# Odd tiles of an expert move into a last step of three tiles, two arms of a branch in every expert step

## The chip, the cores and the metric

One core of one Trainium2 chip runs the whole program in one launch. The metric is the device time of that launch in microseconds (us). One execution was also profiled; its trace gives the start and duration of nearly every instruction. TensorE has two records for a matmul: PEld is the load of the stationary operand, PE the product. Every engine has its own instruction stream with its own branches; registers for the branches are loaded from a small table in SBUF.

## The reference

Attention with random features over 8 batches, 8 heads, 576 tokens of width 64, then a mixture of 8 experts, top 1, over the resulting 4608 tokens of width 512:

```python
x = attention(q, k, v, omega)             # [4608, 512], random-feature (linear) attention
probs = softmax(x @ w_gate)               # [4608, 8]
expert_idx = np.argmax(x @ w_gate, axis=1)
for e in range(8):
    xe = x[expert_idx == e]
    h = np.maximum(xe @ w1[e], 0.0)       # 512 -> 1024
    out[expert_idx == e] = gate_w * (h @ w2[e])   # 1024 -> 512
```

How many tokens an expert gets is known only at run time, so the program has the largest number of steps that could be needed, and leaves by branches.

## The kernel before

**Stages.** Up to about 271 us the core computes the attention, writes x to a DRAM table `token_rows` and counts tokens per expert. From 271 to 297 us it turns the counts into slots (`slots`), gathers the first tokens and computes the first pair of tiles in plain f32 (`fill`, `relu0`, `l20`). From 297 us to the end it runs expert steps.

**Tiles and steps.** The tokens of each expert are padded to tiles of 128. A step t takes two tiles of one expert, 256 tokens. In float32r each product is the sum of three: high part by high part, low weight by high token, high weight by low token. A step is, on TensorE:

1. L1 (`products`, line 869): 8 slices of the hidden width with 12 matmuls each of 128 x 256, 96 in all, into four PSUM banks `p_1`. After each bank ScalarE writes the high part `hh` (line 883) and VectorE the low part `hl` (line 887).
2. `begin(t+1)`: 8 transposes of the next step's gathered tokens (line 850); ScalarE and VectorE split them into `xh` and `xl`.
3. L2 (`l2`, lines 894 to 896): 24 matmuls of 128 x 512 for the first tile and 24 for the second; after each, ScalarE and VectorE scale half of the result by the gate, and GpSimd issues the indirect store to `out` (line 903).

The gathers are indirect DMAs on GpSimd (line 843), two for the step after the next, ahead of the stores.

**Odd tiles.** An expert with an odd number of tiles has a last step with one real tile. L1 still runs over all 256 columns; the second tile's L2 is left out by a branch (`when`, line 908) on a flag loaded in `reg` (line 830), on TensorE, VectorE, ScalarE and GpSimd. Steps 1 to 17 always run; from step 18 on each step is nested in an `If` (`tail`, line 949).

**Slots.** `slots` is a chain on VectorE: counts to tiles per expert, to offsets, to a slot number `f_tt` for each of 36 x 128 tokens, to a one-hot table `f_T` of 36 x NS columns; then 72 small matmuls (line 698) turn that into the token index of each slot, `idx`. While VectorE works on it, TensorE computes `fill(13)`: 13 of the first pair's 32 f32 products (line 797, two records each); ten are done earlier, the last nine by `fill(32)` behind the 72 matmuls. NS is 50. Behind `idx`, VectorE computes the flags (`plan`), splits w1 of the first expert (`split`, line 45) and the tokens of step 1, in that order.

The order of the instructions of each engine is the order in which the code is written.

Of the kernel before, what the change touches and what calls it, by code (L numbers as in the profile page):

```python
# [34 lines left out]
NS = 2 * NPR  # L35
# [376 lines left out]
class Routing:  # L412
# [190 lines left out]
    def head(self, nb, idx, flags):  # L603
# [8 lines left out]
        so, mb, T = t("so", [P, n, E], BF16), t("mb", [P, n]), t("T", [P, n, 2], BF16)  # L612

# [53 lines left out]
    def slots(self, wk, banks, idx, fill):  # L667
# [7 lines left out]
        cnt, c2, off, m = t("cnt", [P, E]), t("c2", [P, E]), t("off", [P, E]), t("m", [P, E, E])  # L675
        c1, tmp = t("c1", [1, E]), t("tmp", [1, E])
# [3 lines left out]
        nc.vector.tensor_scalar(out=tmp, in0=pn[:1, :E], scalar1=float(P - 1), scalar2=1.0 / P, op0=ALU.add, op1=ALU.mult)  # L680
        cb = c2.unsqueeze(1).to_broadcast([P, E, E])
        nc.vector.tensor_tensor(out=m, in0=self.low, in1=cb, op=ALU.mult)
        nc.vector.tensor_reduce(out=off, in_=m, axis=AX.X, op=ALU.add)
        so, tt = self.L.rearrange("p g s e -> p (g s) e"), t("tt", [P, NLT])
        nc.vector.tensor_tensor(out=so, in0=self.OH.rearrange("p g s e -> p (g s) e"),
                                in1=off.unsqueeze(1).to_broadcast([P, NLT, E]), op=ALU.mult)
        nc.vector.tensor_reduce(out=tt, in_=so, axis=AX.X, op=ALU.add)
        nc.vector.scalar_tensor_tensor(out=tt, in0=tt, scalar=2.0, in1=self.RT.rearrange("p g s -> p (g s)"),
                                       op0=ALU.mult, op1=ALU.add)
# [14 lines left out]
        nc.vector.tensor_scalar_add(tmp, tmp, FLOOR)  # L704
        nc.vector.tensor_scalar(out=c1, in0=tmp, scalar1=BIG, scalar2=-BIG, op0=ALU.add, op1=ALU.add)
        self.inc, self.off, self.c1, self.c2 = inc, off, c1, c2

    def plan(self, flags):
# [27 lines left out]
        nc.vector.scalar_tensor_tensor(out=en, in0=self.off[:1], scalar=2.0, in1=self.c1, op0=ALU.mult, op1=ALU.add)  # L736
        nc.vector.tensor_tensor(out=pick, in0=eq, in1=en.unsqueeze(1).to_broadcast([1, NQ, E]), op=ALU.mult)
        nc.vector.tensor_reduce(out=sb, in_=pick, axis=AX.X, op=ALU.add)
        nc.vector.scalar_tensor_tensor(out=sb, in0=self.iop[:1, :NQ], scalar=-2.0, in1=sb, op0=ALU.mult, op1=ALU.add)
        nc.vector.tensor_single_scalar(sb, sb, 1.5, op=ALU.is_gt)  # L740
        for i, a in ((0, ch), (1, nt), (2, act), (4, sb)):
            nc.vector.tensor_copy(flags[:, i, :], a)


class Experts:
# [3 lines left out]
    NC, NF, T2 = DM // P, F // P, 2 * P  # L749
    WE = (ET.DVE, ET.Activation, ET.SP)  # L750

    def __init__(self, tc, ctx, rt, xs, w1, w2, out, ident, ps):
        self.tc, self.nc, self.ctx, self.rt, self.ps, self.ident = tc, tc.nc, ctx, rt, ps, ident
        self.xs, self.w1, self.w2, self.out = xs, w1, w2, out
        cp = ctx.enter_context(tc.tile_pool(name="mo_a", bufs=1))
        self.w1s = cp.tile([P, self.NC, F], F32, name="w1s")
        self.w2s = cp.tile([P, self.NF, DM], F32, name="w2s")
        self.idx = cp.tile([P, NS], U32, name="idx")
        self.x0 = cp.tile([P, self.NC, self.T2], F32, name="x0")
        self.idx0 = cp.tile([P, 2], U32, name="idx0")  # L760
        self.flags = cp.tile([1, 5, NPR + 2], I32, name="flags")
# [5 lines left out]
        gt = cp.tile([P, 6], F32, name="gt")  # L767
        self.gt = [gt[:, i:i + 1] for i in range(6)]
# [71 lines left out]

    def gather(self, t):
        for i in range(2 * t, 2 * t + 2):
            self.nc.gpsimd.indirect_dma_start(out=self.xg[i % len(self.xg)], out_offset=None, in_=self.xs[:, :],
                                              in_offset=bass.IndirectOffsetOnAxis(ap=self.idx[:, i:i + 1], axis=0),
                                              bounds_check=NT - 1, oob_is_err=False)

    def turn(self, i, p):
        x = self.xg[i % len(self.xg)]
        for c in range(self.NC):
            self.nc.tensor.transpose(p[:, c * P:(c + 1) * P], x[:, c * P:(c + 1) * P], self.ident)  # L850
        self.nc.gpsimd.tensor_copy(self.gt[i % 6], x[:, DM:DM + 1])

    def xtrans(self, t):
        nc = self.nc
        for a in range(2):
            p = self.p_x[a]
            self.turn(2 * t + a, p)
            s = slice(a * P, (a + 1) * P)
            split_r(nc, self.xh[t % 2][:, :, s], self.xl[t % 2][:, :, s], p.rearrange("p (c t) -> p c t", t=P),
                    nc.scalar, nc.vector)  # L860

    def products(self, t, g, b):

        NC, T2 = self.NC, self.T2
        h, l = self.xh[t % 2], self.xl[t % 2]
        o = self.p_1[g][:, b * T2:(b + 1) * T2]
        f = slice((2 * g + b) * P, (2 * g + b + 1) * P)
        ops = [(w, h, c) for c in range(NC) for w in (self.w1h, self.w1l)] + [(self.w1h, l, c) for c in range(NC)]
        return [lambda w=w, x=x, c=c, n=n: self.nc.tensor.matmul(o, w[:, c, f], x[:, c, :], start=n == 0,  # L869
                                                               stop=n == len(ops) - 1)  # L870
                for n, (w, x, c) in enumerate(ops)]

    def l1(self, t, g):
        for b in range(2):
            for m in self.products(t, g, b):
                m()

    def hid(self, t, g):
        return (y[t % 2][:, 2 * g:2 * g + 2, :].rearrange("p f t -> p (f t)") for y in (self.hh, self.hl))

    def relu(self, t, g):
        a, b = self.hid(t, g)
        self.nc.scalar.activation(a, self.p_1[g], AF.Relu)  # L883

    def hlow(self, t, g):
        a, b = self.hid(t, g)
        self.nc.vector.scalar_tensor_tensor(out=b, in0=self.p_1[g], scalar=0.0, in1=a.bitcast(F32), op0=ALU.max,  # L887
                                            op1=ALU.subtract)

    def l2(self, t, a):  # L890
        nc, i, k = self.nc, 2 * t + a, slice(a * P, (a + 1) * P)
        h, l, p = self.hh[t % 2], self.hl[t % 2], self.p_2[a]
# [4 lines left out]
        self.store(i, p, self.idx)  # L897

    def store(self, i, p, idx):
        y, c = self.ys[i % 3], DM // 2  # L900
        self.nc.scalar.activation(y[:, :c], p[:, :c], AF.Copy, scale=self.gt[i % 6])  # L901
        self.nc.vector.tensor_scalar_mul(y[:, c:], p[:, c:], self.gt[i % 6])  # L902
        self.nc.gpsimd.indirect_dma_start(out=self.out[:, :], in_=y, in_offset=None, bounds_check=NT - 1,  # L903
                                          out_offset=bass.IndirectOffsetOnAxis(ap=idx[:, i:i + 1], axis=0),
# [21 lines left out]
    def step(self, t, following):  # L926
        for g in range(4):
            if t == 1:
                self.split(2, range(2 * g, 2 * g + 2))
            self.l1(t, g)  # L930
            self.relu(t, g)
            self.hlow(t, g)
        if t + 2 < NPR:
            self.gather(t + 2)
        if t == 1:
            self.next(0, 2)
        following()
        self.nc.gpsimd.drain()  # L938
        self.l2(t, 0)
        self.when(self.reg(4, t, 1, (ET.PE, ET.DVE, ET.Activation, ET.Pool)), lambda: self.l2(t, 1))  # L940
# [11 lines left out]
    def run(self, ctx):  # L952
# [6 lines left out]
        ring = lambda n, sh, dt, k: [cp.tile(sh, dt, name=f"{n}{i}") for i in range(k)]  # L959
        (self.w1h, self.w1l), (self.w2h, self.w2l) = (ring(n, [P, c, w], F32R, 2) for n, c, w in  # L960
                                                      (("w1p", NC, F), ("w2p", NF, DM)))
        self.ys = ring("ys", [P, DM], F32, 3)
        xg = ring("xgm", [P, ROW], F32, 2)
        for x in xg:
            nc.gpsimd.memset(x, 0.0)
        self.xg = self.xg + xg
        self.xh, self.xl = (ring(n, [P, NC, T2], F32R, 2) for n in ("xh", "xl"))
        self.h0 = cp.tile([P, NF, T2], F32, name="h0", tag="hh0")
        self.hh, self.hl = ([cp.tile([P, NF, T2], F32R, name=f"{n}{i}", tag=f"{n}{i}") for i in range(2)]
                            for n in ("hh", "hl"))  # L970

        rt.slots(cp, (self.p_2[0], self.p_x[0], self.p_x[1]), self.idx, lambda: self.fill(13))
# [9 lines left out]
        self.l20(1)  # L982
        self.gather(2)
        for t in range(1, NPL - 1):
# [3 lines left out]
        self.tail(NPL - 1)  # L988
# [45 lines left out]
```

## Time and profile before

| | before |
|---|---|
| time, median of 3 runs | 739.29 us (738.57 to 739.39) |
| the profiled execution's own time | 738.4 us |
| its span, first to last instruction | 736.7 us |
| mean granted TensorE clock | 0.998 |
| busy: PE / DVE / ACT / POOL | 719.9 / 377.9 / 327.5 / 245.7 us |
| expert steps in the trace | 19, two of them with one tile |

The span is 1.7 us short of the execution's own time, which lies at the lower edge of the timed runs; the median is 0.9 us above it. TensorE's records nearly touch each other from start to end, so "busy" for it says that it always had something in flight.

### The profile page before, as it was taken

Reading aid. Unit: us, or ns where it says so; the run is one execution under the profiler, and the core shown is the slowest. Engines: PE = TensorE matmul, PEld = TensorE weight load, DVE = VectorE, ACT = ScalarE, POOL = GpSimd, SP = SyncE. Lnnn points to the kernel's source line nnn. Section 1 sums busy time; section 2 is a strip of 40 time slices with the busy share of each in tenths; the row PEclk is TensorE's granted clock in tenths of the full one; section 3 lists DMA queues with packets and bytes.
Section 4 is the critical chain, followed back from the end, with each engine's and each line's share of the span. In section 5 each row is a group of like instructions: output and inputs, shape, how many; then the busy total and the mean of one; then the engine's idle time right before and its main releaser. Section 6 shows DMA issues by size and latency. Waiting matters only on the chain. (4 is left out here: it accounts for less than half of the span.)

```text
span 736.7 us, 18562 instructions
## 1 busy us (share of the span) xinstructions
PE 719.9 (98%) x7161; PEld 641.1 (87%) x7161; DVE 377.9 (51%) x848; ACT 327.5 (44%) x952; POOL 245.7 (33%) x446
## 2 busy tenths in 40 slices
PE   7999999999999999999999999999999999999996
PEld 6898988888888986898899988998898999889995
DVE  4689898899899887511222153221154217212210
ACT  6878878877778734411122152221152216112210
POOL 7555555555556521322022202122122122201121
PEclk9999999999999999999999999999999999999999
DMA  8944644627444422631011134111026115301000
GB/s 207 256 123 126 201 128 135 195 78 235 144 132 149 177 68 68 216 120 46 28 35 58 59 129 164 44 44 59 19 63 243 45 59 191 134 16 32 30 29 21
DMA packets 68347, 79.34 MB, mean 108 GB/s; under 512 B 27278, under 2 KB 51854, under 8 KB 68240
## 3 DMA queue, kind: packets, MB, share of 16 engines
q1 hardware_dynamic: 61136, 58.81, 25.8%
q0 software_dynamic: 6560, 19.03, 7.6%
q8 instruction: 59, 0.97, 0.6%
q14 instruction: 48, 0.39, 0.2%
q10 hardware_dynamic: 544, 0.13, 0.1%
HBM read 61.06 MB, written 19.55 MB: 109 GB/s over the span
## 5 line engine op out<-in xcount | busy, mean ns | idle before, releaser
L869 PE MATMUL p<-xh,w1p 128*128 128x256 f32 x1216 | 168.1, 280 | 0.3
L869 PEld LDWEIGHTS p<-xh,w1p 128*128 128x128 f32 x1216 | 154.8, 188 | 3.1 <-issue 1.6
L903 POOL DMA_INDIRECT out_dram<-ys,idx x38 | 39.2, 1032 | 347.1 <-DVE ys L902 305.3
L887 DVE SCALAR_TENSOR_TENSOR hl<-p,hh 128x512 fp32r<-128x512 f32 x76 | 52.3, 691 | 145.0 <-ACT hh L883 142.9
L894 PE MATMUL p<-w2p,hh 128*128 128x512 f32 x288 | 115.3, 400 | 0.3 <-PEq L908 0.3
L896 PE MATMUL p<-w2p,hl 128*128 128x512 f32 x288 | 113.6, 395 | 0.0
L895 PE MATMUL p<-w2p,hh 128*128 128x512 f32 x288 | 113.6, 394 | 0.0
L883 ACT ACTIVATE hh<-p 128x512 fp32r<-128x512 f32 x76 | 45.4, 598 | 151.3 <-PE p L869 149.1
L902 DVE TENSOR_SCALAR ys<-p,gt 128x256 f32<-128x256 f32 x38 | 18.3, 483 | 167.0 <-ACT ys L901 167.0
L901 ACT ACTIVATE ys<-p,gt 128x256 f32<-128x256 f32 x38 | 18.0, 474 | 179.2 <-PE p L896 85.3
L869 PE MATMUL p<-xl,w1p 128*128 128x256 f32 x608 | 96.1, 279 | 0.0
L185 ACT ACTIVATE kp<-pp,mx 128x128 f32<-128x128 f32 x256 | 76.2, 417 | 42.9 <-DVE mx L175 22.7
L869 PEld LDWEIGHTS p<-xl,w1p 128*128 128x128 f32 x608 | 82.1, 188 | 0.0
L175 DVE TENSOR_REDUCE mx<-pp 128x8 f32<-128x1024 f32 x64 | 77.0, 1215 | 7.6 <-PE pp L168 4.4
L185 ACT ACTIVATE qp<-pp,mx 128x128 f32<-128x128 f32 x256 | 78.4, 457 | 0.0
L202 POOL TENSOR_TENSOR k<-kp 128x256 f32<-128x256 f32 x64 | 46.7, 729 | 86.3 <-ACT kp L185 77.2
L168 PE MATMUL pp<-om_t,th 64*128 64x128 f32 x1024 | 70.7, 283 | 1.4 <-ACT qp L185 0.7
L168 PEld LDWEIGHTS pp<-om_t,th 64*128 64x128 f32 x1024 | 61.5, 187 | 9.8 <-issue 5.5
L896 PEld LDWEIGHTS p<-w2p,hl 128*128 128x128 f32 x288 | 54.0, 187 | 13.3
L894 PEld LDWEIGHTS p<-w2p,hh 128*128 128x128 f32 x288 | 54.0, 187 | 12.8 <-issue 0.5
L895 PEld LDWEIGHTS p<-w2p,hh 128*128 128x128 f32 x288 | 54.0, 188 | 12.4
L214 DVE COPY qt<-t 128x512 f32<-128x512 f32 x64 | 43.5, 680 | 2.9 <-PE t L212 2.9
(349 smaller groups left out, 1068.3 us busy)
## 6 DMA issues: line engine op xcount, KB each, us to landing
w1s<-in_moe_w_dram SPq DMA_DIRECT2D x5, 2048.0 KB, 9.0
w2s<-in_moe_w_dram SPq DMA_DIRECT2D x5, 2048.0 KB, 10.2
v<-in_v_dram SPq DMA_DIRECT2D x32, 256.0 KB, 5.3
token_rows<-xc SPq DMA_DIRECT2D x8, 1024.0 KB, 5.1
k<-in_k_dram SPq DMA_DIRECT2D x31, 256.0 KB, 5.2
q<-in_q_dram SPq DMA_DIRECT2D x31, 256.0 KB, 5.2
kr<-in_k_dram SPq DMA_DIRECT2D x16, 64.0 KB, 2.6
vz<-in_v_dram SPq DMA_DIRECT2D x16, 64.0 KB, 4.7
```

Of the source, the lines that this page charges most:

```text
L168: nc.tensor.matmul(pp[:, a, n, i, :], th[r, c], self.om[r, :], start=True, stop=True)
L175: nc.vector.tensor_reduce(out=mx[:, :, n], in_=s[("pp", h)][:, :, n], axis=AX.X, op=ALU.max, negate=True)
L185: nc.scalar.activation(x[:, j, :], pp[:, j % 2, n, j // 2, :], AF.Exp, bias=mx[:, j % 2, n, j // 2:j // 2 + 1])
L202: add = lambda o, x, y: nc.gpsimd.tensor_tensor(out=o, in0=x, in1=y, op=ALU.add)
L214: nc.vector.tensor_copy(qt.rearrange("p a b -> p (a b)"), pt)
L869: return [lambda w=w, x=x, c=c, n=n: self.nc.tensor.matmul(o, w[:, c, f], x[:, c, :], start=n == 0, stop=n == len(ops) - 1) for n, (w, x, ...
L883: self.nc.scalar.activation(a, self.p_1[g], AF.Relu)
L887: self.nc.vector.scalar_tensor_tensor(out=b, in0=self.p_1[g], scalar=0.0, in1=a.bitcast(F32), op0=ALU.max, op1=ALU.subtract)
L894: nc.tensor.matmul(p, h[:, c, k], self.w2h[:, c, :], start=c == 0, stop=False)
L895: nc.tensor.matmul(p, h[:, c, k], self.w2l[:, c, :], start=False, stop=False)
L896: nc.tensor.matmul(p, l[:, c, k], self.w2h[:, c, :], start=False, stop=c == self.NF - 1)
L903: self.nc.gpsimd.indirect_dma_start(out=self.out[:, :], in_=y, in_offset=None, bounds_check=NT - 1, out_offset=bass.IndirectOffsetOnAxis(a ...
```

## The change

The steps. A step has two tiles or three. An expert with an odd number of tiles (three or more) has its last three tiles in one step: the rounding of the tiles per expert to steps goes down where the count is odd. Each step loads a flag `two` on all five engines and takes one of two arms: the pair as before, or the three tiles (`third`, then L1 with 384 columns, then three times L2). The third tile has its own slot column (50 + t; NS is 75), gathered into `x3` by one more gather in every step (`gather3`), in the middle of the step before. Its four transposes go into PSUM bank `p_1[3]` at the start of its step. The first slice of the hidden width is computed with 256 columns and then 128, so that the first twelve products do not need the third tile; the other seven slices have 384 columns. Both arms hold everything from L1 to L2, with the next step's gathers, transposes and weight changes.

The buffers `xh`, `xl`, `hh`, `hl` are one each with 384 columns, in place of two each with 256. Steps 1 to 13 always run in place of 1 to 17; from step 14 on each is nested in an `If`.

The slots. VectorE's chain has rows to find the odd experts and the slot of the third tile; two rows behind it go. `fill(13)` becomes `fill(22)`, so that all of the first pair's products lie ahead of the 72 matmuls.

```diff
-NS = 2 * NPR
+NS = 3 * NPR
+NPM = (NT // P - E) // 2
@@ slots
-        nc.vector.tensor_scalar(out=cnt, in0=pn[:, :E], scalar1=float(2 * P - 1), scalar2=0.5 / P, op0=ALU.add, op1=ALU.mult)
-        nc.vector.tensor_scalar_add(cnt, cnt, FLOOR2)
-        nc.vector.tensor_scalar(out=c2, in0=cnt, scalar1=BIG, scalar2=-BIG, op0=ALU.add, op1=ALU.add)
...
+        for c, k, floor in ((c1, P, FLOOR), (c2, 2 * P, FLOOR2)):
+            nc.vector.tensor_scalar(out=cnt, in0=pn[:, :E], scalar1=float(k - 1), scalar2=1.0 / k, op0=ALU.add, op1=ALU.mult)
+            nc.vector.tensor_scalar_add(cnt, cnt, floor)
+            nc.vector.tensor_scalar(out=c, in0=cnt, scalar1=BIG, scalar2=-BIG, op0=ALU.add, op1=ALU.add)
+        nc.vector.scalar_tensor_tensor(out=odd, in0=c2, scalar=2.0, in1=c1, op0=ALU.mult, op1=ALU.subtract)
+        nc.vector.tensor_tensor(out=m, in0=c1, in1=self.least, op=ALU.is_gt)
+        nc.vector.tensor_tensor(out=odd, in0=odd, in1=m, op=ALU.mult)
+        nc.vector.tensor_tensor(out=c2, in0=c2, in1=odd, op=ALU.subtract)
+        nc.vector.tensor_tensor(out=m, in0=c1, in1=odd, op=ALU.mult)
...
+        for v, o in ((off, tt), (m, third)):
+            nc.vector.tensor_tensor(out=so, in0=self.OH.rearrange("p g s e -> p (g s) e"),
+                                    in1=v.unsqueeze(1).to_broadcast([P, NLT, E]), op=ALU.mult)
+            nc.vector.tensor_reduce(out=o, in_=so, axis=AX.X, op=ALU.add)
+        nc.vector.scalar_tensor_tensor(out=third, in0=rt, scalar=1.0, in1=third, op0=ALU.add, op1=ALU.is_equal)
+        nc.vector.scalar_tensor_tensor(out=tt, in0=tt, scalar=2.0, in1=rt, op0=ALU.mult, op1=ALU.add)
+        far = t("far", [P, NLT])
+        nc.vector.tensor_scalar(out=far, in0=tt, scalar1=-0.5, scalar2=float(2 * NPR - 1), op0=ALU.mult, op1=ALU.add)
+        nc.vector.tensor_tensor(out=far, in0=far, in1=third, op=ALU.mult)
+        nc.vector.tensor_tensor(out=tt, in0=tt, in1=far, op=ALU.add)
@@ Experts
+    def gather3(self, t):
+        self.fetch(self.x3, 2 * NPR + t)
...
+    def third(self):
+        self.turn_rows(self.x3, self.p_1[3], self.gt[6])
+        self.columns(2, self.p_1[3])
...
+    def l1(self, t, n):
+
+        for g in range(4 if n == self.T2 else self.NF):
...
+            for k, f in enumerate(range(fs.start, fs.stop)):
+                for c in (slice(0, self.T2), slice(self.T2, n)) if n > self.T2 and g == 0 else (slice(0, n),):
+                    self.products(f, o[:, k, c], c)
...
     def step(self, t, following):
...
+        def between():
+            if t + 2 < NPR:
+                self.gather(t + 2)
+            if t + 1 < NPR:
+                self.gather3(t + 1)
             if t == 1:
-                self.split(2, range(2 * g, 2 * g + 2))
...
+                self.next(0, 2)
+            following()
+            self.nc.gpsimd.drain()
...
+        two = self.reg(5, t, 1, engines + (ET.SP,))
+        with self.tc.If(two > 0) as pair:
+            self.l1(t, self.T2)
+            between()
+            self.l2(t, 0)
+            self.when(self.reg(4, t, 1, engines), lambda: self.l2(t, 1))
+        with pair.Else():
+            self.third()
+            self.l1(t, self.T3)
+            between()
+            for a in range(3):
+                self.l2(t, a)
@@ run
-        rt.slots(cp, (self.p_2[0], self.p_x[0], self.p_x[1]), self.idx, lambda: self.fill(13))
+        rt.slots(cp, (self.p_2[0], self.p_x[0], self.p_x[1]), self.idx, lambda: self.fill(22))
...
-        for t in range(1, NPL - 1):
+        for t in range(1, NPM - 1):
             if t > 1:
                 self.change(t, 2)
             self.step(t, lambda: self.begin(t + 1))
-        self.tail(NPL - 1)
+        self.tail(NPM - 1)
```

The order in which TensorE's instructions stand, at the end of step 1 and the start of step 2. Names: `p_5511` to `p_5514` are PSUM banks of L2, `p_5424` and `p_5426` banks of L1, `w2p` and `w1p` the split weights. Before, the last of the second tile's L2, and L1 of the next step:

```order
L896 MATMUL p_5512<-w2p_5517,hl_5534 128x512
L908 UNCONDITIONAL_BRANCH x2
L869 MATMUL p_5424<-xh_5526,w1p_5515 128x256
L908 UNCONDITIONAL_BRANCH
L869 MATMUL p_5424<-xh_5526,w1p_5516 128x256
```

After, the same place: the end of the pair's arm is followed in the program by the arm of three tiles of the same step.

```order
L922 MATMUL p_5514<-w2p_5520,hl 128x512
L940 UNCONDITIONAL_BRANCH x2
L871 MATMUL p_5429<-ident,x_5533 128x128 x4
L894 MATMUL p_5426<-xh,w1p_5518 128x256
L894 MATMUL p_5426<-xh,w1p_5519 128x256
```

And where that arm of three ends and step 2 begins (188 matmuls, each a load and a product, lie between the two places):

```order
L922 MATMUL p_5513<-w2p_5520,hl 128x512
L972 UNCONDITIONAL_BRANCH
L940 UNCONDITIONAL_BRANCH
L843 TENSOR_LOAD flags
L972 COMPARE_AND_BRANCH
L894 MATMUL p_5426<-xh,w1p_5518 128x256
```

A pair step thus jumps over the whole arm of three, and loads and tests a flag ahead of L1; a step of three jumps over the whole arm of two.

On VectorE, the slot chain from the offsets to the one-hot table. Before (rows named `l_` and `rt_R` belong to the last routing tile and lie between):

```order
L683 TENSOR_REDUCE f_off<-f_m 128x8
L556 TENSOR_SCALAR rt_RT<-l_y 128x5
L685 TENSOR_TENSOR rt_L<-rt_OH,f_off 128x288
L557 SCALAR_TENSOR_TENSOR rt_RM<-rt_RT,l_rk 128x5
L687 TENSOR_REDUCE f_tt<-rt_L 128x36
L560 TENSOR_SCALAR l_nr<-rt_RM 128x5
L561 TENSOR_SCALAR l_nl<-rt_ilo 128x5
L688 SCALAR_TENSOR_TENSOR f_tt<-f_tt,rt_RT 128x36
L692 TENSOR_TENSOR f_T_5565<-f_tt,rt_iop 128x450 x4
```

After:

```order
L690 TENSOR_REDUCE f_off<-f_m 128x8
L694 TENSOR_TENSOR rt_L<-rt_OH,f_off 128x288
L696 TENSOR_REDUCE f_tt<-rt_L 128x36
L694 TENSOR_TENSOR rt_L<-rt_OH,f_last 128x288
L696 TENSOR_REDUCE f_third<-rt_L 128x36
L697 SCALAR_TENSOR_TENSOR f_third<-rt_RT,f_third 128x36
L698 SCALAR_TENSOR_TENSOR f_tt<-f_tt,rt_RT 128x36
L700 TENSOR_SCALAR f_far<-f_tt 128x36
L701 TENSOR_TENSOR f_far<-f_far,f_third 128x36
L702 TENSOR_TENSOR f_tt<-f_tt,f_far 128x36
L705 TENSOR_TENSOR f_T_5593<-f_tt,rt_iop 128x675 x4
```

Between the offsets and the table there are nine rows of the chain in place of three, and the table has 675 elements a row in place of 450. Ahead of the offsets, the chain has 13 rows in place of 6.

## Rows read from the trace of the kernel before

**Rows 1.** The page, section 1: engine, busy us, share, instructions

```profile
PE 719.9 (98%) x7161; PEld 641.1 (87%) x7161; DVE 377.9 (51%) x848; ACT 327.5 (44%) x952; POOL 245.7 (33%) x446
```

**Rows 2.** Busy time by windows: L1, transposes, L2, a pair step, a one-tile step

```profile
367.03:378.34 11.31, 11.31 (x98) 11.31 (x96) 2.56 (x4) 2.27 (x4) 3.38 (x5) 1.00 0.16 56
378.34:379.13 0.79, 0.79 (x11) 0.79 (x9) 0.00 (x0) 0.59 (x2) 0.00 (x0) 1.00 0.00 0
379.13:390.42 11.29, 11.29 (x52) 9.06 (x51) 2.37 (x4) 1.45 (x4) 1.03 (x1) 1.00 0.07 25
390.42:413.80 23.38, 23.38 (x153) 21.16 (x152) 4.93 (x8) 4.31 (x8) 4.41 (x6) 1.00 0.14 46
595.68:613.78 18.10, 17.95 (x129) 16.52 (x128) 8.52 (x14) 8.11 (x16) 3.38 (x5) 1.00 0.14 45
```

**Rows 3.** The page, section 5: groups by line, busy us, mean ns, idle before

```profile
L887 DVE SCALAR_TENSOR_TENSOR hl<-p,hh 128x512 fp32r<-128x512 f32 x76 | 52.3, 691 | 145.0 <-ACT hh L883 142.9
L894 PE MATMUL p<-w2p,hh 128*128 128x512 f32 x288 | 115.3, 400 | 0.3 <-PEq L908 0.3
L883 ACT ACTIVATE hh<-p 128x512 fp32r<-128x512 f32 x76 | 45.4, 598 | 151.3 <-PE p L869 149.1
```

**Rows 4.** Timeline of PE and PEld at the end of a one-tile step

```profile
613.23 0.40 PE L896 MATMUL p<-w2p,hl 128*128 128x512 f32 x1
613.75 0.90 PEld L869 LDWEIGHTS p<-xh,w1p 128*128 128x128 f32 x7 [0.56 <-issue]
```

**Rows 5.** Instructions by line on TensorE's queue: ns min/median/max, first and last start

```profile
L908 PEldq COMPARE_BRANCH  x1: 169/169/169, 386.2 to 386.2; - x1
L908 PEldq COMPARE_BRANCH  x41: 65/169/226, 311.4 to 726.3; - x41
L830 PEldq TENSOR_LOAD <-flags x22: 297/300/481, 310.5 to 720.7; - x22
L949 PEldq COMPARE_BRANCH  x4: 73/130/3892, 680.1 to 731.0; - x4
```

**Rows 6.** The page, section 3: queue, kind: packets, MB, share of 16 engines

```profile
q8 instruction: 59, 0.97, 0.6%
```

**Rows 7.** Timeline of VectorE over the slots: start, us, instruction

```profile
271.38 0.17 DVE L677 TENSOR_SCALAR f_cnt<-p 128x8 f32<-128x8 f32 x1
...
272.40 0.21 DVE L683 TENSOR_REDUCE f_off<-f_m 128x8 f32<-128x64 f32 x1
...
273.65 0.19 DVE L688 SCALAR_TENSOR_TENSOR f_tt<-f_tt,rt_RT 128x36 f32<-128x36 f32 x1
274.10 2.24 DVE L692 TENSOR_TENSOR f_T<-f_tt,rt_iop 128x450 bf16<-128x450 f32 x4 [0.26 <-DVE f_tt L688]
...
278.93 0.21 DVE L700 TENSOR_SCALAR f_lo<-p_x 128x50 f32<-128x50 f32 x1 [1.25 <-PE p_x L698]
...
291.12 1.27 DVE L45 TENSOR_TENSOR xl<-p_x,xh 128x512 fp32r<-128x512 f32 x2
```

**Rows 8.** Timeline of PE over the slots and the first pair

```profile
271.21 5.86 PE L797 MATMUL p<-x,w1s 128*128 128x256 f32 x26
276.90 1.99 PE L698 MATMUL p_x<-f_T,rt_RH 128*128 128x50 bf16 x72
278.73 4.13 PE L797 MATMUL p<-x,w1s 128*128 128x256 f32 x18
282.70 7.03 PE L806 MATMUL p<-w2s,h 128*128 128x512 f32 x16
...
296.91 0.68 PE L869 MATMUL p<-xh,w1p 128*128 128x256 f32 x1
```

**Rows 9.** GpSimd: a gather in the slots, the last store, and waits of the nested exits

```profile
280.13 1.10 POOL L843 DMA_INDIRECT xgm<-token_rows,idx  x1 [5.19 <-DVE f_tmp L704]
732.05 1.00 POOL L903 DMA_INDIRECT out_dram<-ys,idx  x1 [4.57 <-DVE ys L902]
L949 POOLq EVENT_SEMAPHORE  x6: 17/30/1859, 732.5 to 734.7; - x6
```

More of the change, by code (lines that the diff above doesn't have):

```diff
@@ L681, in slots @@
[L681 to L687, printed above, removed]
@@ L688, in slots @@
-        nc.vector.scalar_tensor_tensor(out=tt, in0=tt, scalar=2.0, in1=self.RT.rearrange("p g s -> p (g s)"),
-                                       op0=ALU.mult, op1=ALU.add)
+        cnt, c1, c2, odd, off, m = (t(n, [P, E]) for n in ("cnt", "c1", "c2", "odd", "off", "last"))
+        mm = t("m", [P, E, E])
+        for c, k, floor in ((c1, P, FLOOR), (c2, 2 * P, FLOOR2)):
+            nc.vector.tensor_scalar(out=cnt, in0=pn[:, :E], scalar1=float(k - 1), scalar2=1.0 / k, op0=ALU.add, op1=ALU.mult)
+            nc.vector.tensor_scalar_add(cnt, cnt, floor)
+            nc.vector.tensor_scalar(out=c, in0=cnt, scalar1=BIG, scalar2=-BIG, op0=ALU.add, op1=ALU.add)
@@ new lines, in slots @@
+        nc.vector.tensor_reduce(out=off, in_=mm, axis=AX.X, op=ALU.add)
+        so, tt, third = self.L.rearrange("p g s e -> p (g s) e"), t("tt", [P, NLT]), t("third", [P, NLT])
+        rt = self.RT.rearrange("p g s -> p (g s)")
+        for v, o in ((off, tt), (m, third)):
+            nc.vector.tensor_tensor(out=so, in0=self.OH.rearrange("p g s e -> p (g s) e"),
+                                    in1=v.unsqueeze(1).to_broadcast([P, NLT, E]), op=ALU.mult)
+            nc.vector.tensor_reduce(out=o, in_=so, axis=AX.X, op=ALU.add)
@@ L766, in __init__ @@
         rt.after[3] = rt.head(4, self.idx0, self.flags)
-        gt = cp.tile([P, 6], F32, name="gt")
-        self.gt = [gt[:, i:i + 1] for i in range(6)]
+        gt = cp.tile([P, 7], F32, name="gt")
+        self.gt = [gt[:, i:i + 1] for i in range(7)]
     def ahead(self, k):
@@ L853, in xtrans, with columns @@
+    def columns(self, a, p):
+        s = slice(a * P, (a + 1) * P)
+        split_r(self.nc, self.xh[:, :, s], self.xl[:, :, s], p.rearrange("p (c t) -> p c t", t=P),
+                self.nc.scalar, self.nc.vector)
     def xtrans(self, t):
-        nc = self.nc
         for a in range(2):
[L856 to L888, printed above, removed]
+            self.turn(2 * t + a, self.p_x[a])
@@ new lines, in xtrans, with products @@
+            self.columns(a, self.p_x[a])
+    def third(self):
+        self.turn_rows(self.x3, self.p_1[3], self.gt[6])
+        self.columns(2, self.p_1[3])
+    def products(self, f, o, k):
+        NC, c = self.NC, slice(f * P, (f + 1) * P)
+        h, l = self.xh[:, :, k], self.xl[:, :, k]
+        ops = [(w, h, i) for i in range(NC) for w in (self.w1h, self.w1l)] + [(self.w1h, l, i) for i in range(NC)]
+        for k, (w, x, i) in enumerate(ops):
+            self.nc.tensor.matmul(o, w[:, i, c], x[:, i, :], start=k == 0, stop=k == len(ops) - 1)
@@ new lines, in l1 @@
+    def l1(self, t, n):
+        for g in range(4 if n == self.T2 else self.NF):
+            if t == 1 and g < 4:
+                self.split(2, range(2 * g, 2 * g + 2))
+            p = self.p_1[g % 4]
+            if n == self.T2:
+                fs = slice(2 * g, 2 * g + 2)
+                o = p.rearrange("p (f t) -> p f t", t=n)
+            else:
+                fs = slice(g, g + 1)
+                o = p[:, :n].unsqueeze(1)
+            for k, f in enumerate(range(fs.start, fs.stop)):
+                for c in (slice(0, self.T2), slice(self.T2, n)) if n > self.T2 and g == 0 else (slice(0, n),):
+                    self.products(f, o[:, k, c], c)
+            a, b = self.hh[:, fs, :n], self.hl[:, fs, :n]
+            self.nc.scalar.activation(a, o, AF.Relu)
+            self.nc.vector.scalar_tensor_tensor(out=b, in0=o, scalar=0.0, in1=a.bitcast(F32), op0=ALU.max,
+                                                op1=ALU.subtract)
@@ L926, in step @@
     def step(self, t, following):
-        for g in range(4):
-            if t == 1:
-                self.split(2, range(2 * g, 2 * g + 2))
[L930 to L940, printed above, removed]
+        engines = (ET.PE, ET.DVE, ET.Activation, ET.Pool)
+        def between():
[3 more added lines that the diff above has]
+                self.gather3(t + 1)
+            if t == 1:
+                self.next(0, 2)
[13 more added lines that the diff above has]
+                self.l2(t, a)
     def tail(self, t):
```

63 lines of the change are left out of this document (37 added, 26 removed).

## The prediction

> **What bounds the kernel now.** I read the engines' sums first. TensorE is busy for 719.9 of 736.7 us, the next engine for half as long [rows 1]. The windows of a step confirm it for the expert phase: L1, transposes and L2 of a pair follow each other with TensorE busy for the whole of each window, and VectorE, ScalarE and GpSimd each for under a quarter of it [rows 2]. The groups by line say who waits: ScalarE's first part of the hidden layer sat idle 149.1 us for TensorE's L1, and VectorE's part waited for ScalarE [rows 3]. So in the expert phase a microsecond of TensorE's work, or of a gap in its issue, is a microsecond of time; work on the other engines counts only where TensorE has to wait for it.
>
> How many steps there are follows from counts. Line 883 ran 76 times, 4 to a step, so 19 steps; line 894 ran 288 times, 8 to a tile, so 36 tiles [rows 3]. Two of the 38 places are empty: two one-tile steps.
>
> **Term 1, the steps that go.** With the last three tiles of an odd expert in one step, 36 tiles need 15 pairs and 2 triples, 17 steps. Two one-tile steps of 18.10 us [rows 2] go: -36.2.
>
> **Term 2, two pairs become triples.** A pair's 96 matmuls of 256 columns take 11.31 us, 117.8 ns each; 48 matmuls of 512 columns take 11.29 us, 235.2 ns [rows 2]. That is 0.46 ns a column at both sizes, so I take 176.5 ns for 384 columns. Seven slices of 12 such are 14.82 us. The first slice is 12 of 256 columns, 1.41 us, and 12 of 128. No split product of 128 columns is in the trace; the nearest row is a transpose of 128 columns, 0.79 / 8 = 98.8 ns [rows 2]. By columns it would be 58.9 ns, and at worst as long as 256 columns. I take 98.8, 1.19 us (0.71 to 1.41). L1 is then 17.42 us, 6.11 more than a pair's. Four more transposes add 0.40, 24 more matmuls of L2 add 5.64. A triple is 12.15 us longer than a pair (11.7 to 12.4); two: +24.3.
>
> The third tile's transposes stand at the head of its step, and the split behind them takes about as long as lines 883 and 887, which have the same shape: 0.60 + 0.69 us [rows 3]. The first twelve products, 1.41 us, don't need it, so I cost it at nothing; uncovered it would be up to 0.4 each time. Terms 1 and 2 make -11.9 (-11.4 to -12.8, or 0.8 less if the split shows).
>
> **Term 3, the slots.** Nine products move ahead of the 72 matmuls. They are the 18 records that now stand behind them [rows 8], so TensorE's work is the same; they are cover for VectorE's longer chain. Cover: 26 records take 5.86 us, so 18 take 4.1, and the 72 matmuls could start at 276.90 + 4.1 = 281.0. Chain: from the counts at 271.38 to the offsets at 272.40 five rows pass, 0.20 us each; the offsets to `f_tt`, with two wide rows in it, take 1.25 us [rows 7]. Thirteen more rows, of which two are wide at about 0.5 us, make 11 x 0.20 to 0.26 + 1.0 = 3.2 to 3.9. The one-hot table goes from 50 to 75 columns: 2.24 x 1.5, +1.1. The table, which ended at 276.34, ends at 280.6 to 281.3: the cover and the chain are about even, and I take a wait of 0.2 (0 to 0.6). The 72 matmuls themselves go from 50 to 75 columns. They took 1.99 us [rows 8]; by columns that would be +1.0, by a fixed cost nothing; I take +0.6. Together +0.8 (0 to 1.6).
>
> The chain goes on: `f_lo` at 278.93 moves to about 284.0, and with it the first gather (280.13 [rows 9]), the plan, the split of w1 and last the split of step 1's tokens, which ended at 292.4 [rows 7] and ends at 297.5. TensorE wants to start L1 at 296.91 + 0.8 = 297.7 and reads the low parts of the tokens 8 matmuls later, at 298.6. The cover there is 1.1 us, down from about 5; beyond it each microsecond of chain would be paid.
>
> **Term 4, the extra gather and single buffers.** GpSimd issues one more gather of about 1.1 us a step [rows 9] and is busy for 4.4 of 23.4 us [rows 2]: nothing. `xh` is written again only behind the transposes, which stand behind all of L1; `hh` only behind the next step's first bank, which stands behind all of L2. TensorE's own order covers both: nothing.
>
> **Term 5, the branches.** Each step now has one more flag load and one more branch on TensorE, and a pair step jumps over the arm of three, 388 instructions counted in the program, loads and products apart; a triple's entry jumps over the arm of two, 314. How far ahead the sequencer is: its branch between the second tiles' L2 and the next step was at 386.2, the next L1 started at 390.42 [rows 2, 5], so it runs 4.2 us ahead. A near branch takes 65 to 226 ns and a flag load 0.30 [rows 5], both well inside that lead: nothing, if that is all. But one branch of the four at line 949, the far one out of the nest, took 3.89 us [rows 5]. Its queue of instruction fetches moved 0.97 MB in 59 packets, 16.4 KB each [rows 6]; with 7161 loads and as many products [rows 1], that is one packet for some 243 instructions. So a skip of a one-tile step's L2, 48 instructions, is a fifth of a packet; the far exit, about 1570, six packets; the new skip of 388 is one and a half. The trace has none of this size, so the bounds are: no wait, or 3.89 us at each.
>
> What a wait costs: 3.89, a flag load of 0.30 and a branch of 0.17 behind it, and some 0.3 until TensorE has work again after its queue ran dry (behind a one-tile step the next load began 0.52 us after the last product, 613.23 to 613.75 [rows 4], where a product of L2 takes 0.235); less the lead of 4.2: 0.5 us. Fourteen pair steps are followed by another step. Twelve of these lead to a pair: 0 to 5.8 us. Two lead to a triple, where a second jump follows at once with no lead left: 0.5 to 4.4 each, or nothing, 0 to 8.8. Between ends so far apart, with one and a half packets nearer to a fifth than to six, I take half of the twelve, 2.9, and one and a half waits at each triple, 2.4 each, 4.8: +7.7 (0 to 14.6).
>
> [...]
>
> **Term 6, the end.** Behind the last store, 732.05 + 1.00, GpSimd waits 1.86 us at the exit of the nest [rows 9], since TensorE's far exit began at 731.0 and took 3.89 [rows 5]. The last step is now four levels deep, not two: +0.3 (0 to 0.5).
>
> **Sum.** -11.9 + 0.8 + 7.7 + 0.3 = -3.1 on the profiled execution's 738.4 us: 735.3. The median lies 0.9 above that execution: 736.2 us.
>
> **Rivals.**
> *B, the skips are hidden.* The fetch runs far enough ahead, or the 4.2 us suffice with the flag behind it. For it: near branches never showed, and 3.89 is shorter than the lead. Against: the triples' second jump has no lead. Term 5 is 0: -10.8, 728.5 us.
>
> *C, every skip is waited for: slower.* The place is the first weight load of each step behind a pair's exit. All fourteen wait, both triples twice: 14.6, so +3.8, 743.1 us. It decides once the waits exceed 10.8 us in all, about 0.9 a step; a fetch of two packets in place of one would do it alone. For it: the only far branch in the trace stalled. Against: it jumped four times as far.
>
> *D, the slot chain outlasts its cover.* VectorE's rows take 0.3 us each and not 0.2, the table is late by 1.4 and the token split by 2: TensorE waits at the 72 matmuls and again at L1 of step 1, about 2.5 in all in place of 0.2. -0.8, 738.5 us. For it: the covers of 0.2 and 1.1 us are small. Against: the rows of before ran with others in between, so 0.20 a row is rather long than short.
>
> **How the numbers follow.** 0.2% is 1.5 us, about what a measurement of this kernel can tell. My forecast, some of the skips waiting, net -3.1 within 3.5 either way (732.7 to 739.7): 0.55, of it 0.33 faster, 0.15 same, 0.07 slower. B 0.20, faster. C 0.13, slower. D 0.12: 0.02 faster, 0.06 same, 0.04 slower. Faster 0.55, same 0.21, slower 0.24. The range reaches from B, with a little of the triples' lower bound, to C: 727.5 to 743.5.
>
> **What the profile after would show.** Seventeen steps: the relu's line runs 15 x 4 + 2 x 8 times. A triple step near 35.5 us. The 72 matmuls at about 281 and L1 of step 1 at 297.7. At the start of steps, gaps of about half a microsecond at TensorE's first weight load, put down to issue, at some steps, and of 2 to 4 us ahead of the triples; more instruction packets than 59. Wrong would be: no gaps at all (B), gaps at each step or longer than 0.9 us (C), or L1 of step 1 later than 299 (D). A triple longer than 36.5 us would break term 2.

## The result, and the profile after

The changed kernel takes 743.59 us (median of 12 runs, 737.90 to 747.15) against 739.34 of the kernel before (12 runs, 738.57 to 741.51): ratio 1.0053, interval 1.0034 to 1.0073. It is slower, where 736.2 and faster were forecast; the range ended at 743.5. The profiled execution is one of the longest, 747.14 us with a span of 745.1, so its losses are larger than the median's.

The page after, sections 1 and 3, answers to [rows 1, 6]:

```profile
span 745.1 us, 18502 instructions
PE 712.7 (96%) x6985; PEld 631.2 (85%) x6985; DVE 379.8 (51%) x860; ACT 325.1 (44%) x950; POOL 257.2 (35%) x459
q8 instruction: 83, 1.36, 0.8%
```

TensorE is busy 7.2 us less and the span is 8.4 us longer: it stands still now. The waits of its weight loads at the transposes (`L871`) and at L1 (`L894`):

```profile
PEld p_x L871 <- DMA xg<-token_rows,idx: 7.4, 2, 4.4
PEld p L871 <- issue: 5.0, 2, 3.3
PEld p L894 <- issue: 4.6, 9, 1.1
```

The second and third are term 5, the jumps; the kernel before had none of the second and 1.6 us of the third, at its line 869. The first is new as well and was not forecast. It is in step 1: L1 to L1 takes 33.4 us there, 23.4 in a pair step. The timelines of GpSimd, of SyncE's weight loads and of TensorE's weight loads around it (start, duration, instruction):

```profile
297.29 1.02 POOL L935 DMA_INDIRECT out_dram<-ys,idx  x1 [8.90 <-DVE ys L934]
...
306.30 1.40 POOL L935 DMA_INDIRECT out_dram<-ys,idx  x1 [7.67 <-DVE hl L913]
308.01 1.06 POOL L855 DMA_INDIRECT x<-token_rows,idx  x1 [0.30 <-issue]
309.37 1.06 POOL L855 DMA_INDIRECT xg<-token_rows,idx  x1 [0.30 <-issue]
310.73 0.99 POOL L855 DMA_INDIRECT xg<-token_rows,idx  x1 [0.30 <-issue]
```

```profile
296.74 0.39 SPq L837 DMA_DIRECT2D w1s<-in_moe_w_dram  x1
310.27 0.38 SPq L840 DMA_DIRECT2D w2s<-in_moe_w_dram  x1
```

```profile
313.15 0.72 PEld L871 LDWEIGHTS p_x<-ident,xg 128*128 128x128 f32 x4 [3.04 <-DMA xg<-token_rows,idx]
318.26 0.72 PEld L871 LDWEIGHTS p_x<-ident,xg 128*128 128x128 f32 x4 [4.39 <-DMA xg<-token_rows,idx]
```

Read from the top: the first pair's first store goes out at 297.29, 0.55 us behind a 2 MB load of w1. The second store goes out 9 us later, and behind it on GpSimd the third tile's gather and then the two gathers for step 2. TensorE wants them at 310.1 and gets the first at 313.15; the other was issued 0.46 us behind the 2 MB load of w2 and lands at 318.2, 7.5 us after its issue. In the kernel before, the same gathers went out from 301.0, and a small GpSimd copy in its timeline shows how little was to spare: it waited for the second of them, 0.9 us ahead of the transposes at 308.20. There too the second store came 8.0 us behind the first, 0.9 behind its own data, which were ready at 298.50.

```profile
291.47 1.03 POOL L903 DMA_INDIRECT out_dram<-ys,idx  x1 [8.94 <-DVE ys L902]
...
299.44 1.26 POOL L903 DMA_INDIRECT out_dram<-ys,idx  x1 [6.63 <-DVE w2p L45]
...
302.37 1.28 POOL L843 DMA_INDIRECT xg<-token_rows,idx  x1 [0.31 <-issue]
...
307.32 0.32 POOL L851 COPY gt<-xg 128x1 f32<-128x1 f32 x1 [0.77 <-DMA xg<-token_rows,idx]
```

The stall costs more than its 7.4 us. Windows at the stall and behind it, of the changed kernel (stretch, busy times, then the granted clock and the DMA share):

```profile
309.60:318.26 8.66, 1.83 (x12) 1.23 (x10) 1.93 (x3) 1.18 (x2) 5.01 (x6) 0.70 0.82 280
319.03:323.40 4.37, 4.37 (x13) 3.45 (x12) 0.69 (x1) 0.58 (x1) 0.00 (x0) 0.52 0.29 102
323.40:332.27 8.87, 8.87 (x39) 6.96 (x38) 0.48 (x1) 0.47 (x1) 1.03 (x1) 1.00 0.09 31
```

In the first window, 8.7 us, TensorE was busy for 1.8. Then for 4.4 us the granted clock is 0.52; 13 matmuls take what 18 or 19 take at a granted clock of 1.00 (48 in 11.29 us [rows 2]). In all step 1 is 10.0 us longer than before.

The whole difference of the two spans, by the same places: 1.2 ahead of the slots (the first counts come at 272.4 and not 271.2; the other profiles of this kernel and its variants have 271.6 to 275.5 there, so this differs from run to run); 0.7 from the counts to L1 of step 1 (26.45 for 25.73); 4.8 over the steps, of it 10.0 in step 1; and 1.7 from the last L2 to the end. Sum 8.4.

### The profile page after: what moved, and what is told of

The parts are those of the page before. It is cut to its first block, busy times and chain, and to the rows that moved or that the text cites. A ratio compares the mean times of both kernels' runs of the same rounds, so it can differ in the third digit from the quotient of the medians.

```text
span 745.1 us, 18502 instructions
## 1 busy us (share of the span) xinstructions
PE 712.7 (96%) x6985; PEld 631.2 (85%) x6985; DVE 379.8 (51%) x860; ACT 325.1 (44%) x950; POOL 257.2 (35%) x459
## 3 DMA queue, kind: packets, MB, share of 16 engines
q8 instruction: 83, 1.36, 0.8%
## 4 chain that ended last, share of the span: by engine, by line
PE 38%; DMA 23%; DVE 18%; issue 14%; ACT 4%; POOL 2%; POOLq 1%; SPq 0%; DVEq 0%; ACTq 0%
DMA out_dram<-ys,idx 21%; PE p L894 10%; DVE mx L176 5%; PE p L920 4%; PE p L922 4%; PE p L921 4%; PE pp L169 3%; DVE x L277 3%; DVE qt L215 2%; PE nu L264 2%; PE p L810 2%; PE p L819 2%; DVE rt_RH L593 2%; ACT kp L186 2%; PE tr L149 2%
## 5 line engine op out<-in xcount | busy, mean ns | idle before, releaser
L894 PE MATMUL p<-xh,w1p 128*128 128x256 f32 (+2 forms) x1104 | 159.0, 286 | 1.5 <-ACT ys L933 1.4
L894 PEld LDWEIGHTS p<-xh,w1p 128*128 128x128 f32 x1104 | 145.0, 188 | 5.2 <-issue 4.6
L935 POOL DMA_INDIRECT out_dram<-ys,idx x36 | 37.2, 1033 | 319.3 <-DVE ys L934 223.8
L913 DVE SCALAR_TENSOR_TENSOR hl<-p,hh 128x512 fp32r<-128x512 f32 (+1 forms) x76 | 50.1, 663 | 137.5 <-ACT hh L912 118.8
L912 ACT ACTIVATE hh<-p 128x512 fp32r<-128x512 f32 (+1 forms) x76 | 43.6, 575 | 144.7 <-PE p L894 135.2
L894 PE MATMUL p<-xl,w1p 128*128 128x256 f32 (+2 forms) x552 | 90.2, 285 | 0.0
L894 PEld LDWEIGHTS p<-xl,w1p 128*128 128x128 f32 x552 | 76.7, 188 | 0.0
L264 PE MATMUL nu<-kva,qt 128*64 128x73 f32 x1024 | 43.1, 229 | 3.4 <-ACT kva L251 3.0
```

Source lines behind the costliest of these rows:

```text
L264: nc.tensor.matmul(o[r, j, :], qt[:, j, r], kva[:, a, :], start=True, stop=True)
L894: self.nc.tensor.matmul(o, w[:, i, c], x[:, i, :], start=k == 0, stop=k == len(ops) - 1)
L912: self.nc.scalar.activation(a, o, AF.Relu)
L913: self.nc.vector.scalar_tensor_tensor(out=b, in0=o, scalar=0.0, in1=a.bitcast(F32), op0=ALU.max, op1=ALU.subtract)
```

## The experiments

**e1: the gathers early.** Step 2's gathers and the first third-tile gather stand right behind step 1's:

```diff
         self.gather(1)
+        self.gather(2)
+        self.gather3(1)
...
         self.l20(1)
-        self.gather3(1)
-        self.gather(2)
```

> The changed kernel with step 2's two gathers and the first third-tile gather issued right behind step 1's gathers, ahead of the first pair's two stores on GpSimd. Theory G (the changed kernel loses about 10 us in step 1: the gathers for step 2 queue on GpSimd behind the first pair's second store, which waits until the first store has landed behind the 2 MB weight load; TensorE stands still for 7.4 us and its clock then falls): step 1 takes 23.4 to 23.8 us from L1 to L1 in place of 33.4, no wait of the transposes for a DMA, time 734 to 737 us and a spread under 2 us. Theory S (the loss is the jumps over the other arm and the instruction fetches, and the late gathers only fill time that would be lost anyway): 742 to 744 us.

736.10 us (735.63 to 738.15), ratio to the kernel before 0.9959 (0.9947 to 0.9972): faster than both kernels. Step 1 takes 24.0 us, and no transposes wait for a DMA. Run again on another chip:

> e1 once more, on the same chip as e10, so that the two can be compared: 735.5 to 737.

735.96 (733.52 to 740.23), 0.9968 (0.9950 to 0.9987). G's time held, its spread of 2 us did not.

**e2: the w1 load late,** with the gathers where the change has them.

```diff
         self.split(1)
-        self.next(0, 1)
         self.l20(0)
...
                 self.next(0, 2)
+                self.next(0, 1)
```

> The changed kernel with the load of the second expert's w1 (2 MB) issued in the middle of step 1 behind that of w2, and not ahead of the first pair's first store. The gathers stay where the change has them. Theory G: the first store lands within 3 us, the second is issued at about 300.7 and not 306.3, the gathers for step 2 follow from 302.4 and land by 309, so no wait for a DMA in step 1: 734 to 738 us. If the gathers were late only because of the slot chain, and the first store's landing did not matter, the second store would still be issued at about 306 and the time stay at 742 to 745. Theory S: 742 to 745.

738.03 (736.39 to 743.29), 0.9991 (0.9977 to 1.0006), at the upper edge of what was expected: no transposes wait for a DMA, but step 1 takes 25.9 us, since the jump at its end waits 6.0 (see e10). GpSimd's timeline: the second store now follows the first by 3.6 us and waits only for its data.

```profile
296.58 1.02 POOL L935 DMA_INDIRECT out_dram<-ys,idx  x1 [8.88 <-DVE ys L934]
...
300.20 1.00 POOL L935 DMA_INDIRECT out_dram<-ys,idx  x1 [2.28 <-DVE ys L934]
```

With the load in its old place and the gathers early (e12) the second store still comes 8.5 us behind the first, and the timeline names the first store's landing:

```profile
305.02 1.00 POOL L935 DMA_INDIRECT out_dram<-ys,idx  x1 [7.15 <-DMA out_dram<-ys,idx]
```

So the store waits for the store before it, and that lands late behind the weight load. G holds in both its halves.

**e3 and e8: 13 products ahead of the slots, as before the change,** with the gathers as the change has them (e3) and early (e8).

```diff
-        rt.slots(..., lambda: self.fill(22))
+        rt.slots(..., lambda: self.fill(13))
```

> The changed kernel with 13 products ahead of the slots, as before the change, and nine behind. By the prediction's term 3 the nine products are cover: without them TensorE waits some 4 us for the one-hot table and that is paid in full, 747 us. Theory G: the time of step 1's transposes is set by VectorE's chain and the gathers, not by TensorE; L1 of step 1 starts about 3 us later, the wait for the gathers in step 1 is shorter by as much, and the clock falls less far: 740 to 744 us, no slower than the changed kernel.

> As e1 (early gathers) with 13 products ahead of the slots in place of 22, and nine behind. In e3 the 72 matmuls then started 7.0 us behind the counts, not 9.6, waited 1.1 for the table and ended 1.5 earlier, but L1 of step 1 started 2.4 later. With the gathers early nothing but TensorE counts: 2.4 us slower than e1, 738 to 739. If the earlier slots are worth more than the cover, as e3's gain over the changed kernel suggests: faster than e1.

e3: 738.92 (737.02 to 742.39), 0.9998 (0.9980 to 1.0016), 4.7 below the changed kernel and below what G said. e8: 739.40 (736.43 to 742.85), 0.9998 (0.9984 to 1.0013), 3.3 above e1. TensorE's timeline in e3:

```profile
282.51 3.86 PE L711 MATMUL p_x<-f_T,rt_RH 128*128 128x75 bf16 x72 [1.10 <-DVE f_T L705]
```

The 72 matmuls start 7.0 us behind the counts (275.5 there) and wait 1.1: the table comes in four pieces, and they start with its first. With 22 products ahead they started at 9.6. So `idx` is written 1.5 us earlier in e3, the stores and gathers follow by as much, and L1 of step 1 starts 2.4 later. Both widen the time for the gathers, and the stall is gone: step 1 takes 23.9. The nine early products are worth 3.3 us where the gathers are early and cost 4.7 where they are not.

**e9: no w2 load in step 1.**

```diff
-            if t == 1:
-                self.next(0, 2)
             following()
```

> The changed kernel without the load of the second expert's w2 in step 1, so that the second expert is computed with the first one's w2 and this part of the output is left out. Theory G says that the second of step 2's gathers took 7.5 us and not some 3.5 because that 2 MB load was issued 0.5 us ahead of it. Without it: the wait of the second transposes falls from 4.4 us to about 1.3, the first's stays at 2 to 3, and the clock falls less: 738 to 740 us. If the load did not matter: 742 to 745.

741.21 (740.33 to 742.49), 1.0031 (1.0020 to 1.0042). The waits in its profile:

```profile
PEld p_x L871 <- DMA xg<-token_rows,idx: 3.2, 2, 2.0
```

The second gather's wait falls to 1.2 us, the first's is 2.0, both as expected: the load had held the second up. But the median fell by 2.4 and not by 4 or more. The expectation was taken from the changed kernel's profile, one of its longest executions: from profiled execution to profiled execution it is 5.9 (747.1 to 741.2).

**e6: the kernel before with early gathers.**

> The kernel before with step 2's gathers issued right behind step 1's, as in e1. Theory G: there the gathers for step 2 landed ahead of their transposes, so nothing is gained: 738.5 to 740, ratio 0.999 to 1.001 to the kernel before. If the early gathers were a gain of their own, apart from the change, this kernel would gain too, 3 us or more.

739.29 (738.00 to 740.19), 1.0001 (0.9992 to 1.0010). Nothing: the early gathers only undo what the change brought.

**e4: no branch.** As e1, with the arms fixed for this input:

```diff
-        two = self.reg(5, t, 1, engines + (ET.SP,))
-        with self.tc.If(two > 0) as pair:
+        if t not in (10, 12):
...
-        with pair.Else():
+        else:
```

> As e1 (early gathers), and without the branch on the number of tiles: steps 10 and 12 hold only the three-tile arm and all others only the pair's arm, which is right for this input alone. It shows the price of the branch by itself. By the prediction's term 5 and by the changed kernel's trace (gaps of 0.07 to 0.98 us behind nine exits, 1.48 and 2.97 us ahead of the triples, 7.2 together) it is 7 us faster than e1, 728 to 730 us; the far exit at the end, which took 1.4 us more than before, may give back up to 1.4 of it too. If the jumps cost nothing that is not hidden: as e1.

729.04 (728.40 to 732.25), 0.9871 (0.9853 to 0.9890), 7.1 below e1. Its steps from pair to pair take 23.36 to 23.39 us, as in the kernel before, so the single buffers cost nothing; its page has 57 instruction packets, where those with the arms have 83. Of the 7.1, 1.4 lie at the end (17.9 us from the start of the last L2, 19.2 in e1), which is term 6.

**e7: the flags of steps 1 to 12 in registers ahead of step 1,** on the kernel of e1; run again beside e12.

```diff
+        self.twos = {t: self.reg(5, t, 1, ...) for t in range(1, NPM - 1)}
```

> As e1 (early gathers), with the flags on the number of tiles of steps 1 to 12 loaded into registers ahead of step 1, and not one at the start of each step. Term 5 took a jump that is waited for as 3.9 us, a flag load of 0.30 and a branch of 0.17 behind it, less a lead of 4.2. If so, without the load the exits of steps 1 to 9 fit into the lead: their gaps of 0.07 to 0.3 go, the triples' entries lose 0.3 each, 1.0 to 2.0 us faster than e1: 734 to 735. If the gaps are only the fetch, as e1, 736.

> e7 once more, on the same chip as e12: its profile had 0.1 us of gaps behind the exits of steps 2 to 8 where e1 had 0.7, but its times were no lower than e1's on another chip. By the sum of term 5: 1 to 2 us below e12. If gaps of tenths of a microsecond are made up for elsewhere or lost in the spread: as e12.

737.23 (735.34 to 738.56), 0.9973 (0.9964 to 0.9982), and 737.62 (736.60 to 739.24), 0.9979 (0.9968 to 0.9990), where e12 had 735.96. A miss. The gaps behind steps 2 to 8 went as expected, 0.1 us in all; those ahead of the triples did not shrink. In the second profile step 1's exit waited 5.0 us for its jump (3.8 in e12), and that step took 25.0 us in place of 23.8; and step 12, a triple, took 36.4 in place of 35.1, with a granted clock of 0.78 in its first 6.8 us. Whether the preloading brings either about is not shown: in the first profile these steps took 24.2 and 35.1.

**e10: the arms exchanged,** on the kernel of e1: three tiles in the first arm, the pair in the second.

> As e1 (early gathers), with the two arms exchanged: the three-tile arm stands first, the pair's arm second. A pair then jumps over the other arm at its entry, behind the flag load, and falls through at its end; a triple falls through at its entry, and its end jumps. If the gaps come from a jump of about 3.5 us with a flag load and a branch behind it against a lead of 4.2, a pair's jump at the entry, with the load ahead of it, just about fits (3.5 + 0.5 against 4.2), so gaps behind pairs stay under 0.3; the long gaps of 1.5 and 3 us move from ahead of the triples to behind them, where an exit and an entry jump follow each other; the far exit at the end has one jump and not two. Together 1 to 3 us faster than e1. If only the number of skipped instructions counts: as e1.

747.58 (746.67 to 748.65), 1.0109 (1.0096 to 1.0122), 11.6 above e12: the largest miss. TensorE's L1 waits 16.3 us for issue, 4.0 in e12. One jump is far longer than the rest:

```profile
L972 PEldq COMPARE_BRANCH  x1: 6306/6306/6306, 435.8 to 435.8; - x1
```

The windows of this jump and of one that took 3.29 us (granted clock and DMA share stand ahead of the last number):

```profile
435.80:442.10 6.30, 3.67 (x16) 2.63 (x14) 1.48 (x3) 2.12 (x5) 0.71 (x1) 1.00 0.93 330
...
365.60:368.90 3.30, 3.30 (x15) 2.62 (x15) 0.00 (x0) 0.00 (x0) 0.50 (x1) 1.00 0.23 84
```

The long one falls into a weight load. In e2, where both weight loads run at the end of step 1, the exit there took 6.03 us at a DMA share of 0.94 (the branch, then the window):

```profile
L940 PEldq COMPARE_BRANCH  x1: 6034/6034/6034, 317.4 to 317.4; - x1
```

```profile
317.40:323.40 6.00, 4.30 (x19) 3.12 (x17) 0.48 (x1) 0.47 (x1) 1.03 (x1) 1.00 0.94 371
```

The trace's DMA packets show what is waited for. In each of the changed kernel's eight waits of 3.5 to 3.8 us one packet of the instruction queue, 16.4 KB (1.36 MB in 83 packets), starts 0.9 to 1.5 us behind the branch's start, and the branch ends some 1.4 us behind the packet's end; the exits that take 0.3 to 0.4 have no such packet. In the long waits of e10 and e2 it starts only 3.9 and 3.7 us in. For e10's, the queue from 435.8 to 442.1 and from 439.6 to 442.1 (packets, MB, share):

```profile
q8 instruction: 1, 0.02, 0.9%
...
q8 instruction: 1, 0.02, 2.3%
```

So a gap is the wait less the lead, as term 5 has it, but the wait is no constant: it grows when the packet is late. In e10's jumps of 3.9 to 4.3 us the packet starts 1.5 to 1.9 in, and the one of 5.1 has two packets; why, at DMA shares of 0.2 to 0.4, is open.

**e11: the changed kernel again.**

> The changed kernel itself once more, for a second profile. Its times spread over 9 us where the kernel before spreads over 2. Theory G: the wait for the gathers in step 1 differs from run to run, with the clock that falls behind it, and the rest of the run does not: step 1 takes between 24 and 34 us, and all other steps are within 0.5 us of the first profile except where a gap ahead of a triple lets the clock fall, 1.4 us each.

745.00 (741.43 to 749.26), 1.0076 (1.0048 to 1.0103). In its profile the gathers are waited for 5.1 us, not 7.4, and step 1 takes 31.6. The three-tile step 12 takes 38.2, 3.1 more than in the first profile: as said, a falling clock behind the gap ahead of it (0.64 granted for the step's first 9.5 us), but more than the 1.4. Contrary to the expectation the rest does differ: its counts come at 275.3, 2.9 later than in the first profile.

## Why the prediction was wrong, step by step

**The step that failed** is in term 3: "The chain goes on: ... The cover there is 1.1 us". It followed VectorE's longer chain to the low parts of step 1's tokens and stopped at TensorE's L1. That end held: L1 started 26.45 us behind the counts, 0.7 later than before (0.8 forecast), and did not wait. But the same chain also sets the first pair's scaled outputs, and these the stores on GpSimd. Behind the stores stand the gathers for step 2, the earliest of which waits for the second store, which waits for the first to land, which lies behind the w1 load. Counted from the counts, TensorE moved 0.7 us, this chain 4.7 at `idx` and 7.1 at the first of step 2's gathers, where there was 0.9 to spare. Of the 4.7, 1.5 are the nine products moved ahead (e3); of the 2.4 that came on top, 1.4 are the third tile's gather and 1.0 that the second store stood 9.0 us behind the first, not 8.0. Early gathers (e1, e12) take 7.5 and 9.0 us away, measured against the changed kernel's two medians; the late load (e2) takes 5.6, the earlier slots (e3) 4.7.

Term 4 failed in the same place: the extra gather costs nothing in the steps, but in step 1 it stands ahead of the two that were late, 1.36 us. None of the signs named for B or D showed, and C's, a gap over 0.9 us, only behind steps 15 and 16, where the weight loads idle for 1.1; none of them looked at the transposes of step 1.

**Terms 1 and 2** held. A three-tile step takes 35.49 us from its transposes to the next L1, 35.5 by the sum:

```profile
583.67:619.16 35.49, 35.49 (x192) 32.12 (x193) 12.18 (x21) 10.76 (x21) 5.40 (x7) 1.00 0.26 91
```

e4, which is these two terms with the slots and 0.4 at the end, is 10.2 below the kernel before; the terms gave -11.9 + 0.8.

**Term 5** held in its sum: +7.7 forecast, 7.6 in the profile (1.5 and 3.0 ahead of the triples, 0.8 and 1.0 behind steps 15 and 16, 1.2 behind the others), 5.7 by e4 against e1 without the 1.4 at the end. Eight of fourteen exits jumped with a wait of 3.5 to 3.8 us, seven of them among the twelve that lead to a pair, where half was taken; the others took 0.3 to 0.4. That half was a choice between two bounds, and that it came out is in part luck. Which exits wait is no chance of the run: in all eight profiles with the same arms and flag loads (the changed kernel's two, e1, e12, e2, e3, e8, e9) the exits of steps 1, 4, 5, 7, 8, 11, 15 and 16 wait and the other six do not. Nor does the distance count as the forecast had it: the far exit of the kernel before, 1570 instructions, and these of 388 have one packet each in their wait. Behind steps 15 and 16, in the nest, a second flag load of 0.30 us and the nest's branch follow the exit, which term 5 left out; hence the longer gaps. The branches and the gaps ahead of the triples in the changed kernel:

```profile
L940 PEldq COMPARE_BRANCH  x39: 65/174/3829, 322.5 to 733.0; - x39
...
L972 PEldq COMPARE_BRANCH  x17: 65/77/4837, 292.8 to 714.3; - x17
```

```profile
521.82 0.42 PEld L871 LDWEIGHTS p<-ident,x 128*128 128x128 f32 x4 [1.76 <-issue]
...
583.67 0.42 PEld L871 LDWEIGHTS p<-ident,x 128*128 128x128 f32 x4 [3.25 <-issue]
```

So the traces show a jump of 0.3 to 0.4 us without a packet, or a wait of 3.5 to 3.8 us with one, and of 6.0 and 6.3 where a weight load keeps the DMA busy (shares of 0.94 and 0.93; e2, e10).

**Term 6** was mis-sized: +0.3 forecast, 1.7 measured (19.2 us from the start of the last L2 to the end, 17.5 before). It also misread its row: the branch of 3.89 us [rows 5] began at 726.5 and was over at 730.4, 0.2 ahead of TensorE's last product, and the one at 731.0 is another. So the far exit held nothing up, and GpSimd's wait ended at 734.6, as its last store landed, 2.5 us after its issue at 732.05. In the changed kernel the last step's own exit (3.56 us) stands right ahead of the far one, which takes 5.29, has two packets in it, and ends 4.6 us behind TensorE's last product. The far exit before, and the line after:

```profile
L949 PEldq COMPARE_BRANCH  x1: 3892/3892/3892, 726.5 to 726.5; - x1
```

```profile
L991 PEldq COMPARE_BRANCH  x6: 65/77/5290, 638.7 to 742.3; - x6
```

Without the arms (e4) it took 3.71, was over ahead of the last product again, and the end took 17.9: depth alone costs 0.4. That the late exit makes the other 1.3 is not shown. In the kernels with arms GpSimd goes on 0.7 to 0.9 us behind the last store's last packet, whether the far exit ends late or, as in e10, 3.8 us before that; and in the changed kernel this packet ends 3.2 us behind the store's issue, not 2.1. So the late store stands nearer to the cause; why it is late is open.

**The rivals.** The time is C's, 743.1, the mechanism is not: the jumps cost what the forecast said. B is out by e4. D had the right chain and the wrong end of it: neither the 72 matmuls nor L1 of step 1 waited for VectorE.

**Luck.** With the failed step undone, e1 and e12 take 736.1 and 736.0, and the forecast was 736.2. So close an agreement is in part luck: the jumps cost some 2 us less there than term 5 (by e4), the end 1.4 more than term 6, and terms 1 and 2 gave some 0.5 too much.

**What stays open** is the spread of the changed kernel, 9 us. The two profiles show a stall of 7.4 and of 5.1, and a clock that fell behind a gap ahead of a triple in one run and not in the other; what decides that is not shown. A further part lies ahead of the steps: the counts come at 272.4 in one and 275.3 in the other.

## What to carry to other kernels

When a chain on one engine grows, follow it to every engine that waits for it, not only to the one that bounds the kernel: here the queue behind a store mattered more than the store, for TensorE waited 7.4 us for the two gathers behind it. A copy that waits 0.8 us for a gather, on an engine that counts for nothing, was the row that showed the missing slack. Work moved ahead "as cover" delays what stands behind it: here it cost 4.7 us while a queue of gathers hung on that, and was worth 3.3 once the gathers stood elsewhere.

## What the hardware showed that was not expected

A jump over 388 of TensorE's instructions mostly took 0.3 to 0.4 us or 3.3 to 3.9, in a few cases of e7, e10 and e13 from 1.1 to 5.1, and 6.0 and 6.3 while the DMA share was 0.94 and 0.93; the wait goes with one packet of the instruction queue and its start. A gap did not always cost its own length alone: behind one of 2.68 us in e8 a triple's L1 ran at a granted clock of 0.77 for 6.8 us and its step took 36.5 us in place of 35.1, and much the same in e13 (0.78, 36.4 us), while the gap of 3.25 us above cost nothing behind it. The gap and the window behind it in e8:

```profile
575.64 0.49 PEld L871 LDWEIGHTS p<-ident,x 128*128 128x128 f32 x4 [2.68 <-issue]
```

```profile
576.19:583.00 6.81, 6.81 (x41) 6.81 (x40) 1.25 (x2) 1.34 (x3) 3.38 (x5) 0.77 0.41 123
```
